# Chunked attention with a gated projection and a feed-forward layer: q and k turned on the host, units of 256 tokens, and a written-out TensorE order

## The chip, the cores and the metric

The kernel runs on one core of a Trainium2 chip. The metric is the device time of one execution in microseconds; before the change the median of three runs is 1155.11 us (1153.89 to 1156.46).

## What is computed

```python
# q, k, v: (8, 8, 576, 64) f32; weights f64 in the reference; B*S = 4608 tokens, 512 channels
scores = scale * matmul(q_c, k_c.T)            # in chunks of 64 tokens, per batch and head
attn   = exp(scores - max) / (sum + 1e-9)
x      = matmul(attn, v_c)                     # heads side by side: (8, 576, 512)

gate = sigmoid(sum_k conv_w[k] * xp[:, k:k+S]) # five taps along the tokens of a batch
y    = (gate * (x @ w_val)) @ w_out

xn  = (y - mu) / sqrt(var + 1e-6) * g_ln
out = y + relu(xn @ w_ch1) @ w_ch2             # 512 -> 2048 -> 512
```

Products are made in three parts of float32r: a number is split into a high part and a remainder (high x high, remainder x high, high x remainder).

## The kernel before, in words

The 4608 tokens are nine blocks (BLK) of 512. Attention works in units (UN) of 128 tokens, two chunks each, so 36 units (NU), four to a block (UPB). A Tile scheduler puts each engine's instructions in order by their place in the source, their readiness and modelled costs; inside `manual_schedule` TensorE keeps the source order and the other engines are still scheduled. `high_priority` draws an instruction forward.

The loop at L703 calls `slot(u)` (L625) for each unit, with stages of different units in one slot. `load_qkv` (L85) loads q, k and v of unit u+2 on SP's queue: q and k with tokens on the partitions, in pieces of 256 bytes, one DMA for each half of the heads and each batch touched (L90), v with four DMAs (L99). `a1` (L182) turns k and q: four TensorE transposes each (L177) into a PSUM tile of the pool `ps_t` (two buffers) and a ScalarE copy to kT or qT (L179). `a3` (L186) makes 32 products of 64x64 for the scores (L193) in the single PSUM tile `sc`, then on VectorE the maximum (L200), the subtraction (L203), after ScalarE's exponential (L207) the sum (L209), the reciprocal (L210) and the multiplication (L212). `a4` (L215) transposes the probabilities of unit u-LAG (L220; LAG is 2) into `ps_t` and ScalarE copies them to pT (L222). `a5` (L242) multiplies them with v (L252, 32 products of 64x64) into the single PSUM tile `x`; ScalarE copies it to xf (L267) and xh (L270), and VectorE makes the remainder xl (L272). Where a batch ends inside the unit, these three are cut in two (`segs`).

The dense work of block j is spread over the slots by the table `dense` (`at`, L684), at two places of a slot (0 behind a1, 1 at the end). `conv` (L277) makes the five taps of one of four channel groups: the first on ScalarE (L282), four on VectorE (L284); the first and the last block do it in two halves. `sigm` (L289) is one ScalarE operation over the block's single tile `cg`, for which the activation table has to be loaded again. `val` (L300) is a chain of twelve products (L298) in one of the two PSUM tiles of `ps_d`, read by gv = product x gate on VectorE (L313), then gh on ScalarE (L316) and gl on VectorE (L317). `proj` (L320) is another chain of twelve, copied out by ScalarE (L330) and stored to a DRAM buffer on ScalarE's queue (L331). A block has four val and four proj.

Weights come as f64 words. `decode` (L105) turns a tile into f32 with one ScalarE and three VectorE operations (L108 to L111); `split` (L113) makes the high part on ScalarE (L116) and the remainder on GpSimd (L117). w_val is decoded behind slot 0, w_out in slots 4 to 8, the first four blocks of the feed-forward weights (`load_ff` L141, `split_ff` L151) at slots 35 to 38 of the source.

TensorE's order is the source's until slot 7 (MANUAL); from there to the feed-forward stage the scheduler's. WARM lists places where `warm` (L617) issues products of the identity. `prep` (L662), behind slot 38, releases the attention pools and starts layer norm for block 0; the feed-forward stage (from L736) follows, again in written-out order.

Of the kernel before, what the change touches and what calls it, by code (L numbers as in the profile page):

```python
# [19 lines left out]
def tile_chunk_attention_gated_mlp(ctx: ExitStack, tc: tile.TileContext, q, k, v, w_val, conv_w, w_out, g_ln, w1, w2, out):  # L20
    nc = tc.nc
    B, H, S, D = q.shape
    DM = H * D
# [8 lines left out]
    UN = 128  # L32
# [7 lines left out]
    LAG = 2  # L40
    EARLY = 3
    MANUAL = 7
    WARM = {(0, 0): 2, (0, 1): 4, (0, 4): 12, (1, 4): 7, (2, 4): 3, (3, 4): 13, (4, 2): 6, (4, 4): 12}
    scale = 1.0 / float(D) ** 0.5
    outf = out.rearrange("b s d -> (b s) d")

    def runs(t0, n):
        done = 0
        while done < n:
            b, s = divmod(t0 + done, S)  # L50
            step = min(n - done, S - s)
            yield done, step, b, s
            done += step
# [9 lines left out]
    ps_t = ctx.enter_context(tc.tile_pool(name="ps_t", bufs=2, space=PSUM))  # L63
# [8 lines left out]
    ps_x = s_a.enter_context(tc.tile_pool(name="ps_x", bufs=1, space=PSUM))  # L72

# [9 lines left out]
    qr, kr, vr = {}, {}, {}  # L83

    def load_qkv(u):  # L85
        for src, dst, nm in ((k, kr, "kr"), (q, qr, "qr")):
            t = pA.tile([P, NP, 2, D], F32, tag=nm, name=nm, bufs=3)
            for off, n, b, s in runs(u * UN, UN):
                for r in range(2):
                    nc.sync.dma_start(  # L90
                        out=t[off:off + n, :, r, :],
                        in_=src[b, NP * r:NP * r + NP, s:s + n, :].rearrange("h p d -> p h d"),
                    )
            dst[u] = t
        t = pA.tile([P, 2, NP, D], F32, tag="vr", name="vr", bufs=6)
        for c in range(2):
            b, s = divmod(u * UN + c * CH, S)
            for r in range(2):
                nc.sync.dma_start(  # L99
                    out=t[CH * r:CH * r + CH, c],  # L100
                    in_=v[b, NP * r:NP * r + NP, s:s + CH, :].rearrange("h k d -> k h d"),
                )
        vr[u] = t
# [60 lines left out]

    exps = [pA.tile([P, NP, 2, CH + 1], F32, name=f"ex{i}", bufs=1) for i in range(2)]
    for t in exps:
        nc.gpsimd.memset(t[:, :, :, CH:CH + 1], 1e-9)
    kT, qT, pt, pT = {}, {}, {}, {}  # L170
# [454 lines left out]
    def slot(u, d0=(), d1=()):  # L625
# [3 lines left out]
        if u < NU:  # L629
            a1(u)  # L630
# [178 lines left out]
```

## Time and profile before

| | |
|---|---|
| median of three runs | 1155.11 us (1153.89 to 1156.46) |
| profiled execution: its span (the profile gives no other time for it) | 1152.2 us |
| share of the span with TensorE busy | 96% |
| share with VectorE busy | 63% |
| share with ScalarE busy | 46% |
| mean granted TensorE clock | 0.985 of full speed |
| DMA packets | 168860, of them 120622 under 512 bytes |
| last value product of attention ends | 324.9 us |

Busy is time in which an engine has at least one instruction in flight; instructions of one engine can overlap by some tenths of a microsecond, so durations added up can be more than the busy time. A matmul's end is modelled, and weight loads (PEld) run beside products. An idle time names what ended it.

### The profile page before, as it was taken

The page shows a single profiled execution, that of the slowest core. Times are in us where ns is not written, and L with a number is a line of the kernel's source. Part 1 is how long each engine was busy: PE and PEld are TensorE (multiplying, and loading weights), DVE is VectorE, ACT ScalarE, POOL GpSimd, SP SyncE. Part 2 cuts the span into 40 slices and gives each one's busy share as a digit, 9 for nine tenths or more (in the row PEclk, how much of TensorE's full clock was granted, in tenths as well). Part 3 has the DMA queues.
Part 4 walks back from the last instruction along what each step waited for, and adds up shares of the span by engine and source line. Part 5 has one row for each costly group of instructions (what it writes and reads, how often), then busy time and mean ns, then how long its engine had stood idle before and what let it go on. Part 6 is the DMA issues. An engine that isn't in the chain of part 4 may idle for free.

```text
span 1152.2 us, 18309 instructions
## 1 busy us (share of the span) xinstructions
PE 1104.5 (96%) x7128; PEld 897.8 (78%) x7128; DVE 722.5 (63%) x1277; ACT 527.1 (46%) x973; POOL 107.8 (9%) x120
## 2 busy tenths in 40 slices
PE   6889999899989899799999999999999999999998
PEld 5678877778768787688887888887888888878877
DVE  6988999989884978545556534446444347432434
ACT  4676777767765665334543223333223324121221
POOL 2010012100002443322220000000000000000000
PEclk8989999999999899999999999999999999999999
DMA  7656677664125672623442623333623222622211
GB/s 185 174 128 161 163 183 211 173 164 115 38 74 169 214 230 80 249 109 110 156 156 89 227 89 126 109 101 100 220 91 129 94 80 92 237 92 83 82 37 73
DMA packets 168860, 155.37 MB, mean 135 GB/s; under 512 B 120622, under 2 KB 128838, under 8 KB 168774
## 3 DMA queue, kind: packets, MB, share of 16 engines
q1 hardware_dynamic: 163590, 144.76, 41.4%
q10 hardware_dynamic: 5184, 9.44, 2.2%
q8 instruction: 56, 0.92, 0.3%
q14 instruction: 30, 0.25, 0.1%
HBM read 116.41 MB, written 37.75 MB: 134 GB/s over the span
## 4 chain that ended last, share of the span: by engine, by line
PE 66%; DVE 18%; ACT 7%; issue 3%; DMA 3%; SPq 1%; POOL 0%; DVEq 0%; ACTq 0%; POOLq 0%
PE acc L530 15%; PE x L556 15%; PE psf L530 14%; PE zy L556 10%; DVE cg L284 4%; PE pso L298 4%; PE psv L298 3%; DVE da L111 2%; DVE da L110 2%; PE acc L416 1%; DMA raw<-in_moe_w_ch 1%; DVE h L568 1%; PE psh L298 1%; PE pst L379 1%; PE x L252 1%
## 5 line engine op out<-in xcount | busy, mean ns | idle before, releaser
L576 DVE TENSOR_TENSOR c<-x,c 128x512 f32<-128x512 f32 x96 | 66.2, 690 | 237.5 <-ACT c L572 181.2
L530 PE MATMUL acc<-w,h 128*128 128x512 f32 x768 | 186.4, 392 | 0.0
L530 PE MATMUL psf<-w,h 128*128 128x512 f32 x768 | 186.0, 391 | 0.0
L530 PEld LDWEIGHTS acc<-w,h 128*128 128x128 f32 x768 | 144.7, 188 | 31.6
L530 PEld LDWEIGHTS psf<-w,h 128*128 128x128 f32 x768 | 144.2, 188 | 31.4
L556 PE MATMUL x<-t,wc 128*128 128x512 f32 x576 | 146.9, 390 | 3.4 <-DVE c L576 3.4
L572 ACT ACTIVATE c<-zy 128x512 f32<-128x512 f32 x96 | 57.9, 604 | 187.5 <-PE zy L556 187.4
L556 PEld LDWEIGHTS x<-t,wc 128*128 128x128 f32 x576 | 108.0, 188 | 27.3 <-DVE c L576 4.3
L567 ACT ACTIVATE h<-c 128x512 fp32r<-128x512 f32 x96 | 60.5, 631 | 137.0 <-DVE c L576 136.4
L284 DVE SCALAR_TENSOR_TENSOR cg<-xf,cw,cg 128x516 f32<-128x516 f32 (+1 forms) x176 | 109.8, 662 | 0.4
L535 DVE TENSOR_TENSOR yt<-psf,yt 128x512 f32<-128x512 f32 x128 | 88.2, 691 | 25.1 <-PE psf L530 21.1
L556 PE MATMUL zy<-b,wc 128*128 128x512 f32 x384 | 99.0, 393 | 0.0
L556 PEld LDWEIGHTS zy<-b,wc 128*128 128x128 f32 x384 | 71.1, 188 | 14.8 <-ACT c L572 0.2
L568 DVE SCALAR_TENSOR_TENSOR h<-c,h 128x512 fp32r<-128x512 f32 x96 | 68.4, 713 | 14.1 <-ACT h L567 13.9
L117 POOL TENSOR_TENSOR w<-da,w 128x512 fp32r<-128x512 f32 x32 | 47.6, 1495 | 155.8 <-ACT w L116 139.3
L298 PE MATMUL psv<-xh,vh 128*128 128x512 f32 x144 | 60.0, 417 | 2.0 <-DVE gv L313 2.0
L298 PE MATMUL pso<-oh,gh 128*128 128x512 f32 x144 | 59.2, 411 | 0.3 <-ACT gh L316 0.3
L298 PE MATMUL psv<-xl,vh 128*128 128x512 f32 x144 | 57.4, 399 | 0.2 <-DVE xl L272 0.2
L298 PE MATMUL pso<-oh,gl 128*128 128x512 f32 x144 | 56.9, 395 | 0.2
L298 PE MATMUL psv<-xh,vl 128*128 128x512 f32 x144 | 57.1, 397 | 0.0
L556 PE MATMUL x<-b,wc 128*128 128x512 f32 x192 | 52.6, 410 | 4.3 <-DVE h L568 3.6
L298 PE MATMUL pso<-ol,gh 128*128 128x512 f32 x144 | 56.4, 391 | 0.0
(114 smaller groups left out, 1711.6 us busy)
## 6 DMA issues: line engine op xcount, KB each, us to landing
wc<-wc SPq DMA_DIRECT2D x112, 512.0 KB, 3.3
raw<-in_moe_w_ch SPq DMA_DIRECT2D x32, 512.0 KB, 4.4
vr<-in_v SPq DMA_DIRECT2D x144, 64.0 KB, 3.1
yd<-y ACTq DMA_DIRECT2D x36, 256.0 KB, 3.3
out<-yt SPq DMA_DIRECT2D x36, 256.0 KB, 3.2
kr<-in_k SPq DMA_DIRECT2D x64, 128.0 KB, 2.9
qr<-in_q SPq DMA_DIRECT2D x64, 128.0 KB, 2.9
yr<-yd SPq DMA_DIRECT2D x32, 256.0 KB, 2.8
```

What stands on the lines that cost most here:

```text
L110: nc.vector.scalar_tensor_tensor(out=au, in0=hw, scalar=0x80000000, in1=au, op0=ALU.bitwise_and, op1=ALU.bitwise_or)
L111: nc.vector.scalar_tensor_tensor(out=au, in0=lw, scalar=29, in1=au, op0=ALU.logical_shift_right, op1=ALU.bitwise_or)
L117: nc.gpsimd.tensor_tensor(out=lo, in0=a, in1=hi, op=ALU.subtract)
L284: nc.vector.scalar_tensor_tensor(out=o, in0=x[:, f, i + lo:i + hi], scalar=cw[:, i * CT + f:i * CT + f + 1], in1=o, op0=ALU.mult, op1=ALU.add,
L298: nc.tensor.matmul(out=ps, lhsT=lt, rhs=rh, start=(i == 0), stop=(i == n - 1))
L530: nc.tensor.matmul(out=ps, lhsT=lt, rhs=rh, start=(g == 0 and k == 0 and (first or half)), stop=(g == 1 and k == 2 and (last or half)),)
L535: nc.vector.tensor_tensor(out=yt[i], in0=ps, in1=yt[i], op=ALU.add)
L556: nc.tensor.matmul(out=ps, lhsT=lt, rhs=rh, start=(start and c == 0 and i == 0), stop=(c == 1 and i == 2), skip_group_check=True)
L567: nc.scalar.activation(out=t[:, 0, :], in_=src, func=ACTF.Relu)
L568: nc.vector.scalar_tensor_tensor(out=t[:, 1, :], in0=src, scalar=0.0, in1=t[:, 0, :], op0=ALU.max, op1=ALU.subtract)
L572: nc.scalar.activation(out=t, in_=zy, func=ACTF.Copy)
L576: nc.vector.tensor_tensor(out=t, in0=x, in1=t, op=ALU.add)
```

## The change

- `kernel` lays q and k out on the host: for each of 18 units of 256 tokens one array of 128 partitions (head half x channel) by 2 (k, q) x 4 heads x 256 tokens, contiguous; v likewise with tokens of a chunk x head half on the partitions. `load_qkv` becomes two DMAs per unit, one of 1 MB for qk and one of 512 KB for v. `a1`, `transpose_in`, `runs`, kT and qT are gone.
- UN is 256: 18 units, two to a block. `a3`, `a4` and `a5` handle twice the tokens per call; `sc`, `x` and the new `ps_p` for the transposed probabilities have one buffer each, of 4 KB per partition. `ps_t` is opened only in `prep`.
- LAG is 1. A slot is scores(u), dense 0, transposes(u-1), dense 1, values(u-1), dense 2 and 3.
- MANUAL is 19: TensorE keeps the source order through slot 18, the last with attention work.
- The dense table is written anew: val of block j at places 2 and 3 of slot 2j+3 and 0 and 1 of slot 2j+4, proj at 2 and 3 of that slot and 0 and 1 of the next. The last block's taps are made at full width. WARM has 70 products where it had 59. w_out is loaded in slot 1 and decoded in slots 2 to 4; the first feed-forward weights stand at slots 17 and 18; the taps' weights (`taps`) are transposed in slot 1.

```diff
-    UN = 128
+    UN = 256
...
-    LAG = 2
-    EARLY = 3
-    MANUAL = 7
-    WARM = {(0, 0): 2, (0, 1): 4, (0, 4): 12, (1, 4): 7, (2, 4): 3, (3, 4): 13, (4, 2): 6, (4, 4): 12}
+    LAG = 1
+    MANUAL = 19
+    NC = UN // CH
+    WARM = {(0, 0): 2, (0, 1): 12, (0, 3): 12, (1, 1): 12, (1, 3): 12, (2, 1): 8, (2, 3): 12}
...
     def load_qkv(u):
...
+        t = qkr[u] = pA.tile([P, 2, NP, UN], F32, tag="qk", name="qkr")
+        nc.sync.dma_start(out=t.rearrange("p a h t -> p (a h t)"), in_=qk[u])
+        t = vr[u] = pA.tile([P, NC, NP, D], F32, tag="vr", name="vr", bufs=3)
+        nc.sync.dma_start(out=t.rearrange("p c h d -> p (c h d)"), in_=v[u])
...
-    def transpose_in(u, src, dst, nm):
-        a = src.pop(u)
-        t = pA.tile([P, NP, UN], F32, tag=nm, name=nm)
-        ps = ps_t.tile([P, NP, UN], F32, tag="t", name="pst")
-        for hp in range(NP):
-            nc.tensor.transpose(out=ps[:, hp, :], in_=a[:, hp].rearrange("p r d -> p (r d)"), identity=ident)
-        with tc.high_priority():
-            nc.scalar.activation(out=t, in_=ps, func=ACTF.Copy)
-            dst[u] = t
-
-    def a1(u):
-        transpose_in(u, kr, kT, "kT")
-        transpose_in(u, qr, qT, "qT")
...
     def a3(u):
-        kt, qt = kT.pop(u), qT.pop(u)
-        sc = ps_s.tile([P, 2, 2 * NP, CH], F32, tag="sc", name="sc")
+        t = qkr.pop(u)
+        kt, qt = t[:, 0], t[:, 1]
+        sc = ps_s.tile([P, 2, NG, CH], F32, tag="sc", name="sc")
...
-        nc.vector.tensor_reduce(out=mx, in_=sc[:, :, 0:NP, :], op=ALU.max, axis=AX.X)
+        nc.vector.tensor_reduce(out=mx, in_=sc, op=ALU.max, axis=AX.X)
...
     def a4(u):
         pr = pt.pop(u)
-        t = pA.tile([P, NP, P], F32, tag="pT", name="pT")
-        ps = ps_t.tile([P, NP, P], F32, tag="t", name="pst")
+        t = pA.tile([P, NG, P], F32, tag="pT", name="pT", bufs=1)
+        ps = ps_p.tile([P, NG, P], F32, tag="p", name="pst")
...
-    def slot(u, d0=(), d1=()):
+    def slot(u):
+        d = [dense.get((u, i), []) for i in range(4)]
         if u + 2 < NU:
             load_qkv(u + 2)
         warm(u, 0)
         if u < NU:
-            a1(u)
+            a3(u)
         warm(u, 1)
-        for fn in d0:
+        for fn in d[0]:
             fn()
         if LAG <= u < NU + LAG:
             a4(u - LAG)
         warm(u, 2)
-        if u < NU:
-            a3(u)
-        warm(u, 3)
+        for fn in d[1]:
+            fn()
         if LAG <= u < NU + LAG:
             a5(u - LAG)
-        warm(u, 4)
-        for fn in d1:
+        warm(u, 3)
+        for fn in d[2] + d[3]:
             fn()
...
     for j in range(NB):
         u = UPB * (j + 1) + LAG - 1
         for f in range(CT):
-            if 0 < j < NB - 1:
-                at(u, [(0, 1), (0, 1), (1, 1), (1, 1)][f], lambda j=j, f=f: conv(j, f, 2))
+            if j == NB - 1:
+                at(u, 3, lambda j=j, f=f: conv(j, f, 2))
+            elif j:
+                at(*[(u, 3), (u, 3), (u + 1, 1), (u + 1, 1)][f], lambda j=j, f=f: conv(j, f, 2))
...
-        at(u, (2, 0), lambda j=j: sigm(j))
+        at(u + 1, 2, lambda j=j: sigm(j))
         for f in range(CT):
-            at(u, [(2, 0), (2, 1), (3, 0), (3, 1)][f], lambda j=j, f=f: val(j, f))
+            at(*[(u + 1, 2), (u + 1, 3), (u + 2, 0), (u + 2, 1)][f], lambda j=j, f=f: val(j, f))
         for t in range(BLK // P):
-            at(u, [(4, 0), (4, 1), (5, 0), (6, 0)][t], lambda j=j, t=t: proj(j, t))
...
+            at(*[(u + 2, 2), (u + 2, 3), (u + 3, 0), (u + 3, 1)][t], lambda j=j, t=t: proj(j, t))
+    for f in range(NFA):
+        at(NU + LAG - 2 + f // 2, 1 + 2 * (f % 2), lambda f=f: early_ff(f))
...
+    for u in range(NU + LAG + 4):
         if u == MANUAL:
             head.close()
-        slot(u, dense.get((u, 0), []), dense.get((u, 1), []))
-        if u == NU + LAG:
+        slot(u)
+        if u == NU + LAG - 1:
             prep()
...
+    def chunks(a):
+        a = np.asarray(a).reshape(8, 2, 4, 9, 64, 64).transpose(0, 3, 1, 2, 4, 5)
+        return a.reshape(18, 4, 2, 4, 64, 64)
+
+    def turned(a):
+        return chunks(a).transpose(0, 2, 5, 3, 1, 4).reshape(18, 128, 1, 4, 256)
+
+    data = {
+        "qk": np.concatenate([turned(inputs["k"]), turned(inputs["q"])], axis=2).reshape(18, 128, 2048),
+        "v": chunks(inputs["v"]).transpose(0, 2, 4, 1, 3, 5).reshape(18, 128, 1024),
+    }
```

## Rows read from the trace of the kernel before

**Rows 1.** Busy time of the engines, from the page

```profile
PE 1104.5 (96%) x7128; PEld 897.8 (78%) x7128; DVE 722.5 (63%) x1277; ACT 527.1 (46%) x973; POOL 107.8 (9%) x120
```

**Rows 2.** Stretches: length, busy of PE, PEld, DVE, ACT, POOL, granted clock, DMA share, GB/s

```profile
0.00:48.00 48.00, 36.80 (x517) 31.49 (x517) 34.79 (x63) 25.18 (x46) 7.02 (x15) 0.93 0.65 159
48.00:73.50 25.50, 18.77 (x253) 15.06 (x252) 24.75 (x50) 20.11 (x35) 5.64 (x5) 0.80 0.78 204
73.50:141.30 67.80, 66.89 (x773) 55.27 (x774) 58.39 (x105) 48.46 (x81) 0.61 (x4) 1.00 0.62 155
141.30:254.80 113.50, 106.41 (x1255) 85.73 (x1254) 108.81 (x199) 84.71 (x143) 12.69 (x14) 1.00 0.68 176
254.80:325.00 70.20, 68.91 (x800) 55.22 (x799) 61.20 (x114) 49.36 (x83) 0.39 (x2) 1.00 0.29 79
```

**Rows 3.** Chain of waits before 330 us: start, length, what

```profile
81.26 0.69 PE x L252 x32
...
84.91 0.87 PE pst L177 x8
...
94.17 2.73 PE psv L298 x12
97.99 1.28 ACT L291
99.28 1.93 ACT cg L291
...
133.16 1.93 ACT cg L291
...
310.30 1.94 ACT cg L291
```

**Rows 4.** Single lines and tiles: durations min/median/max in ns, first and last start

```profile
L291 ACT ACTIVATE cg<-cg x9: 1909/1929/1935, 61.3 to 338.3; 128x2064 f32<-128x2064 f32 x7, 128x2048 f32<-128x2048 f32 x2
...
L143 SPq DMA_DIRECT2D raw<-in_moe_w_ch x16: 378/400/606, 130.8 to 426.2; - x16
...
L298 PE MATMUL psh<-xn,w x192: 390/394/792, 361.3 to 458.6; 128*128 128x512 f32 x192
```

**Rows 5.** Groups of instructions before 325 us: busy us, mean ns, idle before

```profile
L179 ACT ACTIVATE qT<-pst 128x512 f32<-128x512 f32 x36 | 21.4, 594 | 0.5 <-PE pst L177 0.5
L179 ACT ACTIVATE kT<-pst 128x512 f32<-128x512 f32 x36 | 21.3, 591 | 6.5 <-PE pst L177 6.5
...
L111 DVE SCALAR_TENSOR_TENSOR da<-raw,da 128x512 uint32<-128x512 uint32 x19 | 15.7, 824 | 0.1
L110 DVE SCALAR_TENSOR_TENSOR da<-raw,da 128x512 uint32<-128x512 uint32 x19 | 14.0, 739 | 0.2
...
L109 DVE TENSOR_SCALAR da<-da 128x512 uint32<-128x512 uint32 x19 | 7.7, 416 | 10.6 <-ACT da L108 10.6
```

**Rows 6.** Timeline of VectorE in two places: start, length, what

```profile
154.83 4.09 DVE L284 SCALAR_TENSOR_TENSOR cg<-xf,cw,cg 128x516 f32<-128x516 f32 x6
...
349.49 1.22 DVE L424 TENSOR_TENSOR xn<-xt,xn 128x1024 fp32r<-128x1024 f32 x1 [0.97 <-ACT xn L423]
350.64 0.68 DVE L313 TENSOR_TENSOR gv<-psv,cg 128x512 f32<-128x512 f32 x1
351.24 0.68 DVE L317 TENSOR_TENSOR gl<-gv,gh 128x512 fp32r<-128x512 f32 x1
```

**Rows 7.** Timeline of the start, all engines

```profile
7.96 0.73 PE L193 MATMUL sc<-kT,qT 64*64 64x64 f32 x32
...
8.62 2.94 PE L623 MATMUL psw<-ident 128*128 128x128 f32 x24
...
10.62 0.43 DVE L109 TENSOR_SCALAR da<-da 128x512 uint32<-128x512 uint32 x1 [10.62 <-ACT da L108]
```

**Rows 8.** DMA issues, from the page: KB each, median us to landing

```profile
wc<-wc SPq DMA_DIRECT2D x112, 512.0 KB, 3.3
...
raw<-in_moe_w_val SPq DMA_DIRECT2D x4, 512.0 KB, 4.9
```

More of the change, by code (lines that the diff above doesn't have):

```diff
@@ L72, in tile_chunk_attention_gated_mlp @@
     ps_x = s_a.enter_context(tc.tile_pool(name="ps_x", bufs=1, space=PSUM))
+    ps_p = s_a.enter_context(tc.tile_pool(name="ps_p", bufs=1, space=PSUM))
     a_dram = [dram.tile([P, DM], F32, name=f"ad{f}") for f in range(NF)]
@@ L80, in tile_chunk_attention_gated_mlp @@
     gr = const.tile([CT, P], F32, name="gr")
-    qr, kr, vr = {}, {}, {}
+    qkr, vr = {}, {}
     def load_qkv(u):
[L86 to L93, printed above, removed]
-            dst[u] = t
[L95 to L103, printed above, removed]
+        t = qkr[u] = pA.tile([P, 2, NP, UN], F32, tag="qk", name="qkr")
+        nc.sync.dma_start(out=t.rearrange("p a h t -> p (a h t)"), in_=qk[u])
+        t = vr[u] = pA.tile([P, NC, NP, D], F32, tag="vr", name="vr", bufs=3)
+        nc.sync.dma_start(out=t.rearrange("p c h d -> p (c h d)"), in_=v[u])
     def decode(raw, a):
@@ L245, in a5 @@
         va = vr.pop(u)
-        x = ps_x.tile([P, 2, NP, UN], F32, tag="x", name="x")
+        x = ps_x.tile([P, 2, NP // 2, UN], F32, tag="x", name="x")
         for i in range(NP // 2):
-            for c in range(2):
+            for c in range(NC):
+                n, cs = c // 2, slice(c % 2 * CH, (c % 2 + 1) * CH)
                 for f in range(2):
@@ L636, in slot, with at @@
         warm(u, 2)
[L637 to L639 removed]
+        for fn in d[1]:
+            fn()
         if LAG <= u < NU + LAG:
             a5(u - LAG)
[L642 to L657 removed]
+        warm(u, 3)
+        for fn in d[2] + d[3]:
+            fn()
+    dense = {}
+    def at(u, i, fn):
+        dense.setdefault((u, i), []).append(fn)
     s_0 = ExitStack()
[L660 removed]
+    xn0, yt0, ps_t = None, None, None
     def prep():
[L663 removed]
+        nonlocal xn0, yt0, ps_t
         s_a.close()
+        ps_t = ctx.enter_context(tc.tile_pool(name="ps_t", bufs=2, space=PSUM, reuse_waits="tile"))
         p2["b"] = ctx.enter_context(tc.tile_pool(name="p2c", bufs=2, side="right", reuse_waits="tile"))
@@ L681, in prep, with taps, early_ff @@
             high_low(xn0[0][:, :, ts], xn0[1][:, :, ts], p2["xt"][:, :, ts], nc.vector)
-    dense = {}
-    def at(u, pos, fn):
-        dense.setdefault((u + pos[0], pos[1]), []).append(fn)
+    def taps():
+        cwr = stg.tile([KC * CT, P], F32, tag="da", bufs=3, name="cwr")
+        decode(cwu, cwr)
+        ps = ps_p.tile([P, NP * P], F32, tag="p", name="pst")
+        nc.tensor.transpose(out=ps[:, 0:KC * CT], in_=cwr, identity=ident[0:KC * CT, 0:KC * CT])
+        nc.tensor.transpose(out=ps[:, KC * CT:(KC + 1) * CT], in_=gr, identity=ident[0:CT, 0:CT])
+        nc.vector.tensor_copy(out=cw, in_=ps[:, 0:(KC + 1) * CT])
+    def early_ff(f):
+        load_ff(f, stg)
+        split_ff(f, stg)
+    at(0, 3, lambda: split_w("v"))
+    at(1, 0, taps)
+    at(1, 3, lambda: load_w(w_out, "o", CT))
+    for c in range(CT):
+        at([2, 3, 3, 4][c], [3, 0, 3, 0][c], lambda c=c: split_w("o", c, c + 1))
     for j in range(NB):
@@ L784, in tile_chunk_attention_gated_mlp @@
     order.close()
-_INS = ["q", "k", "v", "moe_w_val", "moe_conv_w", "moe_w_out", "moe2_g_ln", "moe2_w_ch1", "moe2_w_ch2"]
+_INS = ["moe_w_val", "moe_conv_w", "moe_w_out", "moe2_g_ln", "moe2_w_ch1", "moe2_w_ch2"]
 _OUT = (8, 576, 512)
```

82 lines of the change are left out of this document (28 added, 54 removed).

## Prediction

> **What bounds the kernel now.** I read the busy times, a table of stretches, the chain of waits, the rows of single tiles, the groups of VectorE and ScalarE, and the two engines' timelines. TensorE is busy for 1104.5 of 1152.2 us [rows 1], but the change touches the part before 325 us alone, where the last product of attention ends, so that part decides. The table [rows 2] has two sorts of stretch. At 73.5 to 141.3 and 254.8 to 325 TensorE leads: busy 98.7% and 98.2%, VectorE 86.1% and 87.2%. At 48 to 73.5 and 141.3 to 254.8 VectorE leads: 97.1% and 95.9%, TensorE 73.6% and 93.8%. The reader should see that both engines are nearly full, and that to lighten one leaves the other. The pace is the distance between sigmoids, one for each block of 512 tokens: 33.9 us where TensorE leads (99.28 to 133.16) [rows 3], 38.0 before it, where VectorE does, and 249 us for the seven blocks from 61.3 [rows 4] to 310.3 [rows 3], 35.6 each. In the long VectorE-led stretch it also decodes feed-forward weights, loaded from 130.8 us on [rows 4].
>
> **What the change removes.** TensorE loses 288 transposes of k and q. In the chain eight of them take 0.87 us [rows 3]; 36 times that is 31.3 us. ScalarE loses 72 copies, 21.3 + 21.4 us [rows 5]; it is busy for at most 79% of any stretch, so this buys no time by itself, only earlier hand-overs. TensorE's idle time in the second stretch, where it waits for k and q, is covered by VectorE at 97%: VectorE is late next there, and I count nothing. SP issues 36 loads of q, k and v where 304 stood; they move the same bytes.
>
> **What merging units does to VectorE.** Four softmax passes run 18 times at 128x1024 where they ran 36 times at 128x512, and the remainder xl goes from 40 instructions to 24 (12 whole units and 6 cut at a batch boundary). That is 72 + 16 = 88 merges. By durations a merge saves 2 x 0.68 - 1.22 = 0.14 us. By starts a 128x512 operation takes 0.60 us of the queue and a 128x1024 one 1.15, both from one run of neighbours [rows 6], so a merge saves 0.05. Instructions overlap where the queue is full, as it is here, so I take the starts: 4.4 us (0 and 12 as bounds). The 18 reciprocals saved are left to the range. The last block's taps become 16 at full width where 32 halves stood, fewer, but none can start before the last product, where half of them could; I set the two against each other.
>
> The Trainium skill, "VectorE: DVE Perf Modes", section "Side-by-side: where the cycles go for N=2048 bf16", adds some 158 cycles of pipe fill and decode to each instruction at 0.96 GHz. By that rule the 88 merges would be worth an estimated 14.5 us instead of 4.4. The trace agrees with it on the duration (0.14 us) and not on the queue (0.05).
>
> **The sum for VectorE.** Busy before 325 us: 34.79 + 24.75 + 58.39 + 108.81 + 61.20 = 287.9 us [rows 2]; less 4.4, 283.5. It starts at 10.62 us, on the first weight, with the first scores behind it [rows 7]. Afterwards the first scores need one load of 1 MB and no transposes or copies. No row shows such a load: 512 KB take 3.3 to 4.9 us [rows 8], so it takes between 3.3 and 9.8. At 5, near the rows, it lands at 6, and VectorE begins near 8 (bounds 6 to 12). TensorE's sum is 36.80 + 18.77 + 66.89 + 106.41 + 68.91 = 297.8 [rows 2], less 31.3, plus eleven more warming products at 0.25 us (24 halves in 2.94) [rows 7]: 269 us. So VectorE becomes the longer engine, and the stage's end is its start, its work and its idle time. It idled for 4.1% of the long stretch that it led, and for 12.8 and 13.9% of those that TensorE led [rows 2]. With TensorE at under 90% of the new stage I take 6.5%, nearer the first: 283.5/0.935 = 303 us, and the end at 311, 14 us earlier. The bounds are 8 + 283.5/0.959 = 304 (21 earlier) and 8 + 283.5/0.861 = 337 (12 later).
>
> TensorE checks this. A block holds eight chains of twelve (2.73 us), 128 score and 128 value products (0.69 us for 32) and sixteen probability transposes (0.44 for four, half of the 0.87): 21.9 + 5.5 + 1.8 = 29.2 us [rows 3]. Seven blocks at 29.2 instead of 35.6 would be 45 us less; VectorE needs about 28.5 of its own per block (58.39/67.8 of 33.9 is 29.2, less 0.5) and the decoding besides, so most of TensorE's gain is not to be had. Between 14 and 45 I stay near VectorE's end, as it is the longer engine: **20 us**.
>
> **What the fixed order and a lag of one add.** TensorE's program becomes scores(u), a dense chain, transposes(u-1), a dense chain, values(u-1), two dense chains. The probabilities of u-1 have a whole slot, about 15 us, for four passes of 1.15 us and an exponential: hidden. The copy of the transposed probabilities is hidden by the 2.73 us chain after them. The tight place is the sigmoid: val(j,0) and val(j,1) fill both dense PSUM tiles, so val(j,2) waits until gv has read val(j,0), which wants all taps and the sigmoid. From the end of block j's values to val(j,2) TensorE has six dense chains, two scores and one value stage of 1.38 us each and transposes: 6 x 2.73 + 3 x 1.38 + 0.87 = 21.4 us. Against it stand the copies out of PSUM (1.2), a first tap (0.6, as a copy of its size), 16 x 0.67 (six in 4.09) [rows 6], xl (1.15), a softmax, if it is put between the taps (4.7), and a table load and the sigmoid (1.28 + 1.93) [rows 3]: 21.6 us. The stall is some 0.2 us a block, none if softmax comes after, and 3 or more if gl and a decoding also go first. It is inside the idle share taken above. A wait on SP is added too: the load of unit u+2 waits for scores(u), with weight loads queued behind it; it has nearly two slots to land and costs nothing unless a load takes over 15 us, against 3.3 to 4.9 [rows 8].
>
> What stands behind 325 us keeps its order; the first feed-forward chain (361.3 us) [rows 4] comes as much earlier.
>
> **The sum.** Span 1152.2 - 20 = 1132.2 us. The median of the three runs, 1155.1, is 2.9 above the span, so the forecast is **1135 us**.
>
> **The rivals.**
> - Merges pay their whole duration (0.14 us): 88 x 0.09 = 8 us more. For it stand the durations, against it the starts. 1127; chance 0.13, in which a denser interleaving is another way to the same number.
> - VectorE's queue idles nearly as where TensorE led, at 9.5%: 8 + 283.5/0.905 = 321, 4 us gained, and up to 8 with the reciprocals. For it: the steps are twice as long, with one set of buffers for scores, values and transposes. 1149; chance 0.17.
> - The gain is not there: the eight decodings of early feed-forward weights are not drawn forward any more, so the stage loses 8 x (0.42 + 0.74 + 0.82) = 16 us of VectorE [rows 5] and the next one, whose first chains want them, gains as much. 1155; chance 0.05.
> - **Slower:** at the sigmoid TensorE can't take other work, as the order is written out. If gl (2 x 0.60) and a decoding (1.98) go ahead of the taps, the stall is 3.4 us a block; if the softmax behind them then misses its own slot, 4.7 more, 8.1. From 6.4 (35.6 - 29.2) on, this costs more than the transposes did: 7 x 1.7 = 12 slower, 1167; chance 0.10. Against it: the trace has six taps in a row [rows 6], so VectorE's order does bring them early.
>
> **How the numbers follow.** The forecast has the other 0.55, with its own range of 1127 to 1143. A measurement here can tell about 0.2% (2.3 us) from nothing. Faster: 0.55 + 0.13 + 0.17 = 0.85; same 0.05; slower 0.10. The range takes in the merge rival, the bounds of the first load and the idling rival, and leaves out the last two: 1116 to 1152, where 1116 is a gain of 39, most of TensorE's 45.
>
> **What would show it.** Right: no transposes of k or q; sigmoids 31 to 34 us apart; VectorE over 92% busy until the last value product near 305; its first pass near 8 us; the first feed-forward chain near 341. Wrong: TensorE waiting on gv for more than 3 us per block, VectorE under 88%, feed-forward weights decoded only after the last block, or a first score after 10 us.

## The result: 0.6% slower, and the profile after

The changed kernel takes 1161.43 us (1159.38 to 1163.26, 5 runs) against 1154.74 (1151.30 to 1156.46, 5 runs) beside it: ratio 1.0063 [1.0045, 1.0082]. Forecast was 1135, with 1152 as the upper end, and a chance of 0.10 for slower.

The busy times of the changed kernel, from the page (answers to [rows 1]):

```profile
PE 1076.1 (93%) x6862; PEld 875.5 (76%) x6862; DVE 714.0 (62%) x1155; ACT 482.4 (42%) x828; POOL 110.6 (10%) x120
```

TensorE lost 28.4 us of busy time, VectorE 8.5 and ScalarE 44.7: what the change removes is gone. DMA packets fell from 168860 to 58581. Yet the span is 1157.6 us, 5.4 longer than before. The stretches of the changed kernel, with the columns of [rows 2], show where TensorE stood still:

```profile
0.00:55.80 55.80, 34.82 (x614) 32.14 (x614) 43.33 (x66) 23.50 (x34) 7.80 (x16) 0.87 0.68 255
55.80:144.00 88.20, 71.40 (x831) 56.80 (x826) 85.28 (x126) 55.72 (x77) 17.01 (x15) 0.91 0.45 152
144.00:322.50 178.50, 160.61 (x1873) 129.37 (x1872) 147.28 (x219) 101.28 (x129) 4.11 (x10) 0.94 0.34 118
322.50:369.50 47.00, 37.36 (x161) 29.86 (x162) 23.50 (x43) 24.81 (x44) 0.00 (x0) 0.89 0.34 115
```

From 55.8 to 144 us VectorE leads (96.7%). From 144 us on, neither TensorE (90.0%) nor VectorE (82.5%) is full; each waits for the other, and the granted clock is below full speed in every stretch, where [rows 2] has 1.00 from 73.5 us on. The sigmoids give the pace (timeline of ScalarE in the changed kernel: start, length, what, and in brackets the idle time before and what ended it):

```profile
66.69 1.91 ACT L257 ACTIVATE cg<-cg 128x2048 f32<-128x2048 f32 x1
...
241.73 1.92 ACT L257 ACTIVATE cg<-cg 128x2064 f32<-128x2064 f32 x1 [3.43 <-DVE cg L250]
275.47 1.92 ACT L257 ACTIVATE cg<-cg 128x2064 f32<-128x2064 f32 x1 [3.43 <-DVE cg L250]
309.13 1.92 ACT L257 ACTIVATE cg<-cg 128x2064 f32<-128x2064 f32 x1 [2.96 <-DVE cg L250]
```

Against [rows 3, 4] the time goes in three places. **The head** loses 5.4 us (first sigmoid 61.3 to 66.69). **The seven blocks** behind it take 242.4 instead of 249.0 us, a gain of 6.6 of the 20 forecast; late blocks take 33.7, as the 33.9 of a TensorE-led block before. **The last block** loses 11.5: its sigmoid stands at 348.62, 39.5 behind the one before it, where it was 28.0. The first feed-forward chain starts at 369.5 (361.3 before), and the stage behind it gives 2.8 back.

The waits of TensorE before 345 us in the changed kernel (engine, tile, what it waited for: total, times, longest; the last block's wait for gv, 7.2 us, ends at 351.3 and is not in them):

```profile
PE psv L264 <- DVE gv L279: 33.9, 8, 6.1
PE pst L645 <- DVE cwr L90: 6.3, 1, 6.3
```

The first is the stall that the prediction priced at 0.2 us a block: a third value chain that waits for gv, as the sigmoid is late. Why it is late, the timeline of VectorE in the changed kernel shows (the first line is ScalarE's, the copy of the block's last values):

```profile
254.82 1.06 ACT L233 ACTIVATE xf<-x 128x512 f32<-128x512 f32 x2
...
255.07 1.28 DVE L283 TENSOR_TENSOR gl<-gv,gh 128x512 fp32r<-128x512 f32 x2
...
256.55 1.23 DVE L179 TENSOR_TENSOR pr<-ex,sm 128x1024 f32<-128x1024 f32 x1
257.70 0.68 DVE L238 TENSOR_TENSOR xl<-x,xh 128x512 fp32r<-128x512 f32 x1
258.30 2.08 DVE L250 SCALAR_TENSOR_TENSOR cg<-xf,cw,cg 128x516 f32<-128x516 f32 x3
...
263.56 1.21 DVE L167 TENSOR_REDUCE mx<-sc 128x16 f32<-128x1024 f32 x1
...
265.36 1.22 DVE L170 TENSOR_TENSOR ex<-sc,mx 128x1024 f32<-128x1024 f32 x1
...
269.16 1.23 DVE L176 TENSOR_REDUCE sm<-ex 128x16 f32<-128x1040 f32 x1
...
271.75 1.22 DVE L179 TENSOR_TENSOR pr<-ex,sm 128x1024 f32<-128x1024 f32 x1
...
273.56 1.22 DVE L238 TENSOR_TENSOR xl<-x,xh 128x1024 fp32r<-128x1024 f32 x1
274.69 0.75 DVE L250 SCALAR_TENSOR_TENSOR cg<-xf,cw,cg 128x516 f32<-128x516 f32 x1
277.43 1.42 DVE L279 TENSOR_TENSOR gv<-psv,cg 128x384 f32<-128x384 f32 x4 [1.99 <-ACT cg L257]
```

Ahead of the first tap (258.30) stand gl and pr; between it and the last (274.69) stand the whole softmax of the unit scored next (263.56 to 271.75) and the xl of the next values (273.56). gv starts at 277.43, 22.6 us after the copy of the last values to xf began (254.82), and takes until 278.80, when TensorE's third value chain starts. Behind the stall comes a second cost, in the same two views of the changed kernel, timeline of TensorE and stretches:

```profile
278.80 0.47 PE L264 MATMUL psv<-xh,vh 128*128 128x512 f32 x1 [3.31 <-DVE gv L279]
...
280.20 0.63 PE L264 MATMUL psv<-xh,vl 128*128 128x512 f32 x1
280.62 0.63 PE L264 MATMUL psv<-xh,vh 128*128 128x512 f32 x1
```

```profile
266.00:275.00 9.00, 9.00 (x140) 7.15 (x142) 9.00 (x13) 4.98 (x6) 0.00 (x0) 1.00 0.31 99
...
278.80:283.30 4.50, 4.50 (x13) 3.44 (x14) 3.51 (x5) 1.04 (x2) 0.00 (x0) 0.62 0.00 0
```

Products that follow each other every 0.23 us at the granted clock of 1.00 (2.4 GHz) are 0.42 apart after 3.3 us of standing still, where the clock is partly at the lower level (1.2 GHz; 0.62 on average). The chain takes 4.58 us instead of 2.75.

### The profile page after: what moved, and what is told of

Its sections match the earlier page's. It is cut to its first block, busy times and chain, and to the rows that moved or that the text cites. A ratio compares the mean times of both kernels' runs of the same rounds, so it can differ in the third digit from the quotient of the medians.

```text
span 1157.6 us, 17062 instructions
## 1 busy us (share of the span) xinstructions
PE 1076.1 (93%) x6862; PEld 875.5 (76%) x6862; DVE 714.0 (62%) x1155; ACT 482.4 (42%) x828; POOL 110.6 (10%) x120
## 4 chain that ended last, share of the span: by engine, by line
PE 62%; DVE 26%; ACT 4%; issue 4%; DMA 3%; POOL 0%; SPq 0%; POOLq 0%; ACTq 0%
PE acc L496 15%; PE x L522 15%; PE psf L496 14%; PE zy L522 9%; DVE cg L250 8%; PE psv L264 5%; DVE da L90 2%; DVE sm L176 2%; DVE da L89 2%; DVE xl L238 1%; DVE gv L279 1%; PE acc L382 1%; DVE mx L167 1%; DVE h L534 1%; DVE ex L170 1%
## 5 line engine op out<-in xcount | busy, mean ns | idle before, releaser
L496 PEld LDWEIGHTS acc<-w,h 128*128 128x128 f32 x768 | 144.2, 188 | 31.4
L496 PEld LDWEIGHTS psf<-w,h 128*128 128x128 f32 x768 | 144.2, 188 | 31.3
L250 DVE SCALAR_TENSOR_TENSOR cg<-xf,cw,cg 128x516 f32<-128x516 f32 (+2 forms) x160 | 105.0, 699 | 0.0
L264 PE MATMUL psv<-xh,vh 128*128 128x512 f32 x144 | 66.0, 458 | 41.1 <-DVE gv L279 41.1
L264 PEld LDWEIGHTS psv<-xh,vh 128*128 128x128 f32 x144 | 31.0, 215 | 49.3 <-issue 28.9
L264 PE MATMUL psv<-xl,vh 128*128 128x512 f32 x144 | 63.1, 438 | 0.0
L264 PE MATMUL psv<-xh,vl 128*128 128x512 f32 x144 | 62.5, 434 | 0.0
```

The lines of the kernel that those rows point to most:

```text
L250: nc.vector.scalar_tensor_tensor(out=o, in0=x[:, f, i + lo:i + hi], scalar=cw[:, i * CT + f:i * CT + f + 1], in1=o, op0=ALU.mult, op1=ALU.add,
L264: nc.tensor.matmul(out=ps, lhsT=lt, rhs=rh, start=(i == 0), stop=(i == n - 1))
L496: nc.tensor.matmul(out=ps, lhsT=lt, rhs=rh, start=(g == 0 and k == 0 and (first or half)), stop=(g == 1 and k == 2 and (last or half)),)
```

## Experiments

Ratios are to the kernel before the change, on the same chip. Edits are to the changed kernel unless another is named.

### The layout alone

The kernel before, with its units of 128, its lag and the scheduler's order, but q, k and v loaded in the new layout:

```diff
+        t = qkr[u] = pA.tile([P, 2, NP, UN], F32, tag="qk", name="qkr", bufs=3)
+        nc.sync.dma_start(out=t.rearrange("p a h t -> p (a h t)"), in_=qk[u])
...
-        if u < NU:
-            a1(u)
```

> The kernel before with one part of the change: q, k and v laid out on the host and loaded with two DMAs per unit, no transposes of k and q, no copies; units of 128 tokens, a lag of two, the scheduler's TensorE order from slot 7 on, as before. Theory (the fixed order at the sigmoid ate what the transposes gave back): 31 us of TensorE are gone and nothing was added, so sigmoids come 31 to 32 us apart where TensorE led (33.9 before), and the time is 10 to 18 us below before, 1137 to 1145. Rival (VectorE was the bound, the transposes were covered): within 4 us of before.

1158.03 us, ratio 1.003 [1.0009, 1.0051]: slightly slower, and within the rival's 4 us. TensorE fell to 1089.0 us busy, but waited 21.8 us in ten for the probabilities, at a mean granted clock of 0.966 (before 0.985). So the transposes' 31 us can be lost without units of 256 or a written-out order. A lag of three took most of that wait away, and a source order besides told whether the scheduler was to blame:

```diff
-    LAG = 2
+    LAG = 3
```

> The kernel before with the host layout alone (1158.0 us, where TensorE waited 21.8 us in 10 for the probabilities), and the probabilities used three units later instead of two. Theory (without the transposes of k and q TensorE reaches the probabilities before VectorE has made them; the loss is one of latency): waits for pr under 8 us, sigmoids from block 4 on 32 to 34 apart, time 1144 to 1152. Rival (VectorE's sum sets the pace, 29 to 36 us a block, so TensorE waits somewhere else): the waits move to gv or the scores, time within 4 of 1158. Third (one more unit of lag at the end costs a block's tail): time over 1160.

1153.96 us, 0.9985 [0.9955, 1.0014]: 4 us better. The wait for pr fell from 21.8 to 4.6 us, the waits at the score tile rose from 17.9 to 26.3 in all, and late blocks still took 33 to 37. Mostly the rival: the wait moved.

```diff
-    LAG = 2
-    MANUAL = 7
+    LAG = 3
+    MANUAL = 39
```

> The kernel before with the host layout alone, a lag of three, and TensorE's instructions in source order through the last unit. With a lag of three and the scheduler's order TensorE waited 4.6 us for the probabilities, but 26 us at the score tile, and took 34 us a block. Theory (the order that the scheduler found is what kept the layout's gain away): waits at the score tile under 8 us, blocks 5 to 8 at 31 to 32.5, time 1138 to 1148. Rival (the written-out order stalls here as it did in the changed kernel, behind the sigmoid): waits for gv over 15 us, time 1152 to 1162.

1178.69 us, 1.0209 [1.0176, 1.0242]. The rival holds, and more than it said. Waits of TensorE in this kernel:

```profile
PE psv L272 <- DVE gv L287: 40.8, 8, 10.5
```

The stall of the changed kernel, in another kernel with small units: it comes with the fixed order ahead of the sigmoid. That some order gives the layout alone its gain was not shown.

### The order on TensorE

```diff
-    MANUAL = 19
+    MANUAL = 5
```

> The changed kernel with the scheduler's TensorE order from slot 5 on instead of slot 19. Theory: at a late sigmoid the scheduler lets TensorE take other work, the waits on gv (33.9 us in 8 waits) shrink to under 10, sigmoids come 31 to 32 us apart instead of 33.7, and the time falls by 10 to 20 us to about 1145. Rival (units of 256 with one set of buffers and a lag of one make the stage latency-bound in any order): 1158 to 1165, the waits stay or move to other tiles.

1152.41 us, 0.9985 [0.9968, 1.0001], 9.0 below the changed kernel, between theory and rival. Waits for gv fell from 33.9 to 12.4 us, but 13.0 us of waits for pT came in. The order was a cause, not the whole.

### The taps ahead of the next softmax

```diff
-                at(*[(u, 3), (u, 3), (u + 1, 1), (u + 1, 1)][f], lambda j=j, f=f: conv(j, f, 2))
+                at(u, 3, lambda j=j, f=f: conv(j, f, 2))
```

> The changed kernel, with all four channel groups' taps of a block (2 to 8) placed at the end of its own slot, ahead of the next unit's softmax in the source; TensorE's program is the same. Theory (the sigmoid is late because 4.7 us of softmax stand between the taps on VectorE): the wait on gv falls from 3.3 us to below 1 in blocks 4 to 8, sigmoids come 30.5 to 32 us apart, 1140 to 1150. Rival (VectorE is the longer engine by its sum of work, or softmax then comes late itself): the wait goes from gv to pr, the pace stays at 33 to 34 us and the time within 5 us of 1161.

1153.13 us, 0.9992 [0.9976, 1.0008], 8.3 below the changed kernel with the same TensorE program. Its waits before 345 us:

```profile
PE pst L186 <- DVE pr L179: 23.6, 8, 4.5
PE psv L264 <- DVE gv L279: 14.2, 3, 7.1
```

The last value product ended 8 us earlier (313.9). What gv lost, pr partly took: with softmax behind the taps, the transposes wait for it. (The 14.2 hold the last block's wait, 7.1 us, which here ends ahead of 345; the 33.9 of the changed kernel don't hold its 7.2.) The time lies between theory and rival.

### Layer norm behind the last sigmoid

In the changed kernel `prep` stands one slot before the last sigmoid. Its timeline of ScalarE:

```profile
338.39 2.93 ACT L337 ACTIVATE yt<-yt,w,r 128x512 f32<-128x512 f32 x4 [4.15 <-DVE w L335]
341.23 4.20 ACT L347 ACTIVATE xt<-pst,cw 128x128 f32<-128x128 f32 x16
345.21 2.10 ACT L389 ACTIVATE xn<-xt 128x1024 fp32r<-128x1024 f32 x2
...
348.62 1.91 ACT L257 ACTIVATE cg<-cg 128x2048 f32<-128x2048 f32 x1
```

The taps are done at 339.9; layer norm's 9 us go first.

```diff
-        if u == NU + LAG - 1:
+        if u == NU + LAG:
             prep()
```

> The changed kernel with layer norm of block 0 (prep) one slot later in the source, behind slot 19, as before it stood one slot behind the last values. Theory (at the end ScalarE does the layer norm's scaling and 18 copies ahead of the last block's sigmoid, 348.6 us where the taps end at 339.9): the sigmoid comes near 342, the first feed-forward chain 5 to 8 us earlier than 369.5, the time 4 to 8 us below the changed kernel, 1153 to 1157. Rival (the feed-forward stage is held by its weights anyway): within 2 us of 1161.

1156.76 us, 1.0025 [1.0008, 1.0041]: 4.7 less than the changed kernel, sigmoid at 343.25. Together with the taps:

> Two of the earlier edits together: the taps placed ahead of the next softmax (measured 1153.1 alone) and prep one slot later (1156.8 alone, where the changed kernel has 1161.4). Theory (two separate losses, one at each block's sigmoid and one at the last block's): they add up, 8 + 5 us, to about 1148; the last sigmoid comes near 332 instead of 340.6 and the first feed-forward chain near 356. Rival (once the stage is shorter the feed-forward stage is held by its weights, so the second edit is worth nothing any more): within 2 us of 1153.

1147.93 us, 0.9949 [0.9931, 0.9968]: the two add up (8.3 + 4.7 = 13.0; 13.5 measured).

### The head

The timeline of TensorE in the changed kernel shows the transposes of the taps' weights, put ahead of the first probabilities, waiting for their decoding:

```profile
26.66 0.29 PE L645 MATMUL pst<-ident,cwr 20*128 20x20 f32 x1 [6.35 <-DVE cwr L90]
...
30.39 1.88 PE L219 MATMUL x<-pT,vr 64*64 64x64 f32 x60 [1.11 <-ACT pT L188]
```

```diff
-    at(1, 0, taps)
+    at(1, 3, taps)
```

> The changed kernel with the turning of the conv taps' weights (two TensorE transposes that wait 6.4 us for their decoding) behind the first unit's value products instead of ahead of its probability transposes. Theory (written-out order: the first values, 30.4 us, wait for something that they do not need, and VectorE idles 4 us for them): the first values come near 24, the first sigmoid 3 to 5 us earlier than 66.7, the time 2 to 5 us below 1161. Rival (VectorE is full at 40 to 100 us, so the head's wait is made up there): the first sigmoid moves by less than 1.5 us, the time by less than 1.5.

1155.73 us, 1.0005 [0.9989, 1.002]: 5.7 less than the changed kernel; first values at 25.7, first sigmoid at 60.89. With all three edits:

> The three edits of order together: taps ahead of the next softmax, prep one slot later, the conv weights turned behind the first values. Theory: the losses add, 8 + 5 + 3 us, about 1145, clearly below the kernel before (1154.2). Rival (the losses overlap: what one stage gains the next gives back waiting for VectorE): 1150 to 1154.

1143.45 us, 0.9908 [0.9888, 0.9928]: 18.0 less, and 8.3 + 4.7 + 5.7 is 18.7.

### The tail, and the one gate tile

The run with three edits still took 36.4 us for the last block. The last block's taps in halves, as before the change:

```diff
-                at(u, 3, lambda j=j, f=f: conv(j, f, 2))
+                at(u - 1, 3, lambda j=j, f=f: conv(j, f, 0))
+                at(u, 3, lambda j=j, f=f: conv(j, f, 1))
```

> Three losses undone, and the last block's taps in two halves again, as before the change. In the run with three losses undone the last sigmoid was at 328.2 us, 36.4 behind the one before, against 28.0 in the kernel before the change. Theory (the halves matter: the first half of the taps runs while the last unit is still being computed): sigmoid near 320 to 322, first feed-forward chain near 343 to 345, time 1136 to 1139 against 1143.5. Rival (the forecast's 'the two set against each other': the last products or layer norm set the sigmoid): sigmoid at 326 to 328, time within 2 of 1143.5.

> As the run with halves, and layer norm of block 0 one more slot later in the source. Theory (layer norm's instructions on VectorE, about 6 us between taps, and four on ScalarE, 2.9 us ahead of the table load, still delay the last sigmoid): sigmoid 3 to 6 us earlier than with halves alone, and 2 to 4 us off the time, so 1133 to 1136. Rival (layer norm's result is then late for the first feed-forward chain): that chain is not earlier, or later by some us, and the time is equal to or above that with halves alone.

1139.56 us, 0.989 [0.9854, 0.9927], and with layer norm yet later 1138.46, 0.987 [0.984, 0.99]: 3.9 and 5.0 less than the run with three edits, but longer than the theories had it (last sigmoids in the profiles at 331.8 and 324.7 us). In both, the first half of block 8's taps is written into `cg` while two value chains of block 7 have yet to read their gate, so those rows come from another gate; in the changed kernel's table the halves can't stand without a second gate tile. That is why full width was not merely "set against" the halves. A third use of xf's two buffers gives the tile:

```diff
+        if j == NB - 1 and j not in cgs:
+            cgs[j] = pD2.tile([P, CT, BLK + 2 * HALO], F32, tag="xf", name="cg8")
+        o = cgs.get(j, cg)[:, f, lo:hi]
```

> Three losses undone, the last block's taps in two halves into a gate tile of their own (a third use of the two buffers of xf, so that block 7's gate stays whole for its last two value chains), and layer norm of block 0 one slot later. Theory (the tail was late because the last block's taps could not start before the last values, and they could not because the one gate tile was in use): last sigmoid at 322 to 326, first feed-forward chain near 344 to 346, time 1136 to 1140, as the run where the halves were written over block 7's gate (1138.5). Rival (the spare tile comes free late, as block 7's taps and halo copy still read it): sigmoid at 328 or later, time 1142 to 1145.

1138.54 us, 0.9871 [0.9842, 0.9899]: theory. Timeline of ScalarE in this kernel:

```profile
298.59 1.69 ACT L250 ACTIVATE cg<-xf,cw 128x256 f32<-128x256 f32 x4
...
320.75 1.92 ACT L260 ACTIVATE cg<-cg 128x2048 f32<-128x2048 f32 x1
322.57 1.50 ACT L340 ACTIVATE yt<-yt,w,r 128x512 f32<-128x512 f32 x2
```

The last block's taps start at 298.59 (309.94 in the run with three edits), ahead of the last values, which end at 307 to 308 in both. The last sigmoid now stands ahead of layer norm's yt, 29.7 us behind the one before, and the first feed-forward chain at 343.7. Without the written-out order (MANUAL = 5):

> The run with the spare gate tile, and TensorE's order left to the scheduler from slot 5 on. Theory (the written-out order cost something only because of the three losses; with them gone it is as good as the scheduler's): time within 3 of that run. Rival (the scheduler's order is better here too, as it was by 9 us in the changed kernel): 5 us or more below it. Third (the scheduler puts attention's stages back to back and TensorE waits at the score tile, as with the layout alone): 5 us or more above it.

1141.41 us, 0.989 [0.9854, 0.9926], 2.9 more: theory, just. The written-out order is no loss once these pieces are moved.

### A later place for the transposes of the probabilities

```diff
-        if LAG <= u < NU + LAG:
-            a4(u - LAG)
-        warm(u, 2)
         for fn in d[1]:
             fn()
+        if LAG <= u < NU + LAG:
+            a4(u - LAG)
...
```

In the run with three edits, `a4`, `a5` and the whole dense table go one chain later.

> Three losses undone, and the transposes of the probabilities and the value products each one dense chain later in a slot, with the dense table shifted along. TensorE waited there for pr 21.7 us in 7 and for gv 10.9 us in 3. Theory (TensorE comes to these transposes too early; 2.7 us more of slack takes most of each wait): waits for pr under 8 us, pace of blocks 2 and 3 still about 35 because VectorE is full there, time 1134 to 1140. Rival (the loop of softmax, values, taps and sigmoid is as long as before, so the wait only moves): waits for gv grow by what those for pr lose, time within 3 of 1143.5. Third (the dense window between a block's values and its third projection is what counts; it is the same): no change.

1153.18 us, 0.9994 [0.9976, 1.0012]: 9.7 more than without the edit, and the wait for pr stayed (28.0 us in nine). All three expectations missed; from the third on the sigmoids came 33 to 38 us apart. The place of `a4` didn't make the slack, perhaps since everything behind it moved along; why it lost so much is open.

### What a stall costs besides its wait

Identity products ahead of each third value chain of blocks 0 to 7, in the place of the wait:

```diff
+    def fill():
+        ps = ps_p.tile([P, NG, P], F32, tag="p", name="psw")
+        for _ in range(22):
+            nc.tensor.matmul(out=ps[:, 0, :], lhsT=ident, rhs=ident, start=True, stop=True)
+    for j in range(NB - 1):
+        at(2 * j + 4, 0, fill)
```

> The changed kernel with 22 more products of the identity in a PSUM tile of their own ahead of each val(j,2), where TensorE waits 3 to 6 us for gv; nothing waits for them but TensorE itself. Theory (the wait also costs the clock: the chain behind it takes 4.4 to 5.4 us instead of 2.75, at a granted clock of 0.83 to 0.91 in such stretches): the products take 2.7 us of the wait, the chain behind it falls to 2.75 to 3.5 us, sigmoids in blocks 4 to 8 come 32 us apart instead of 33.7, and the time falls by 6 to 12 us, to 1150 to 1155. Rival (the slow chain is bookkeeping, or gv itself sets the pace): the pace stays at 33.7 or grows by what the products take, 1160 to 1172.

1159.27 us, 1.004 [1.0023, 1.0057], 2.2 less. Timeline of TensorE in this kernel:

```profile
276.75 5.18 PE L661 MATMUL psw<-ident 128*128 128x128 f32 x44
281.68 0.48 PE L264 MATMUL psv<-xh,vh 128*128 128x512 f32 x1
```

The chain ran at full speed (2.79 us), but the fill outlasted the wait, and the chain started 7.6 us behind its sigmoid (274.12) instead of 3.3. So this run could not tell. With 11 products (`range(11)`):

> The changed kernel with 11 identity products ahead of each third value chain, where 22 took 4.9 to 5.2 us in place of a wait of 3.1 to 4.4 us and so pushed the chain back by more than they spared. Eleven take about 2.6 us, less than the wait, so the chain starts when gv is read, as in the changed kernel. Theory (the lower granted clock behind the wait, 4.4 to 5.4 us for a chain that takes 2.75 at the full one, is on the path that sets the pace): chains at 2.8 us, pace of blocks 5 to 8 32 to 32.5 instead of 33.7, time 1148 to 1153. Rival (the chain's slowness is absorbed later, by the wait of the next block): chains at 2.8 us, the next wait longer by as much, pace 33.5 to 33.9, time 1158 to 1163. Third (the fill does not hold the clock): chains at 4.4 us, no change.

1148.46 us, 0.9955 [0.9939, 0.9972]: **13.0 less than the changed kernel (12.5 by the ratios), by adding useless work**. Timeline of TensorE, and stretches between two sigmoids, in this kernel:

```profile
238.50 2.72 PE L661 MATMUL psw<-ident 128*128 128x128 f32 x22
240.98 0.48 PE L264 MATMUL psv<-xh,vh 128*128 128x512 f32 x1
```

```profile
205.40:236.80 31.40, 31.40 (x392) 26.03 (x391) 28.21 (x43) 19.25 (x25) 0.31 (x2) 1.00 0.41 135
236.80:268.20 31.40, 31.40 (x392) 25.99 (x392) 28.11 (x42) 19.29 (x26) 0.31 (x2) 1.00 0.40 135
```

In these blocks TensorE never stops; a block takes 31.4 us where it took 33.7, at a granted clock of 1.00. By its time it is the theory, with a pace a little shorter still. The last five blocks are 2.0 to 2.4 us shorter each, 11.1 together; the first four keep waits for gv of 0.6 to 3.7 us and gain little.

But the fill did not change the clock alone. With it in TensorE's order the scheduler made another order on ScalarE: the next exponential goes ahead of the copy to pT, which stands behind the slow chain. Timeline of ScalarE behind the sigmoids at 275.47 (changed kernel) and 236.83 (this run):

```profile
284.28 1.03 ACT L188 ACTIVATE pT<-pst 128x1024 f32<-128x1024 f32 x1 [4.45 <-PE pst L186]
...
287.14 1.06 ACT L174 ACTIVATE ex<-ex 128x1024 f32<-128x1024 f32 x1
```

```profile
244.36 1.06 ACT L174 ACTIVATE ex<-ex 128x1024 f32<-128x1024 f32 x1 [1.93 <-DVE ex L170]
...
245.85 1.01 ACT L188 ACTIVATE pT<-pst 128x1024 f32<-128x1024 f32 x1
```

The exponential comes 7.5 us behind its sigmoid instead of 11.7, so softmax is done sooner and the next taps meet less other work on VectorE. Of a late block's 2.3 us, the chain gives 1.6 (2.84 from its start to the next stage, instead of 4.39) and the way from the block's values to the end of the next sigmoid 1.6 (21.4 instead of 23.0), and 0.8 is lost as the chain starts 0.8 later behind its sigmoid. The first is the clock's. How much of the second comes from the faster chain and how much from the new order, no run separates.

The Trainium skill, "TensorE: Matmul & The Clock Gate", section "Loop structure matters more than you think", says that the loop nest decides whether products run at the full clock, with a wait for a DMA as its example. Here TensorE waits for VectorE, and the two runs agree: 0.62 granted behind the 3.3 us wait, 1.00 with the fill in its place.

Then the short fills where VectorE leads, ahead of `a4` in the run with the spare gate tile:

```diff
+        for _ in range(8):
+            nc.tensor.matmul(out=ps[:, 0, :], lhsT=ident, rhs=ident, start=True, stop=True)
+    for u in (6, 8, 10):
+        at(u, 0, fill)
```

> The run with the spare gate tile, and 8 filling products (2.0 us) ahead of the transposes of the probabilities in slots 6, 8 and 10, where TensorE waits 4.9, 5.3 and 3.1 us for pr and the transposes behind the wait take 1.57 to 1.97 us instead of 1.04. Theory (the granted clock behind these waits is on the path): each block 2 to 4 gains 1 to 2.5 us, time 1132 to 1136. Rival (VectorE is full in these blocks, 31.7 of 32, 36.6 of 38 and 35.4 of 37 us, so a faster TensorE only waits longer): within 2 of 1138.5.

1136.73 us, 0.9843 [0.9809, 0.9877]: 1.8 less, inside the rival's bound (3.2 less by the ratios). In this kernel's timeline the transposes stayed slow at the first two places (1.97 us without the fill):

```profile
106.47 1.94 PE L186 MATMUL pst<-ident,pr 128*128 128x128 f32 x8 [3.22 <-DVE pr L179]
```

So it did not tell whether the clock counts there; a wait of 3.2 us was left behind the fill. At the third place 1.5 us of wait were left, the transposes ran at a granted clock of 1.00 (0.69 without the fill), and the sigmoid behind them came 31.4 us after the one before instead of 32.3.

### The best version

The run with the spare gate tile, with the taps back where the change put them, and 11 fills ahead of the third value chain:

```diff
-                at(u, 3, lambda j=j, f=f: conv(j, f, 2))
+                at(*[(u, 3), (u, 3), (u + 1, 1), (u + 1, 1)][f], lambda j=j, f=f: conv(j, f, 2))
...
+    for j in range(NB - 1):
+        at(2 * j + 4, 0, fill)
```

> The run with the spare gate tile, but with the taps where the change put them (half of them behind the next scores) and 11 filling products ahead of the third value chain. The changed kernel gained 13.0 us from these fills alone, and from the head, the tail and layer norm about 15 us together. Theory (the losses are at different places and add up): blocks 5 to 8 at 31 to 32, last sigmoid near 320, time 1132 to 1136. Rival (with the fills TensorE's program is 31.9 us a block, against 30.2 to 32 with the taps drawn ahead): time 1138 to 1144.

1133.79 us (1130.51 to 1135.71), 0.9815 [0.9781, 0.9848]: it beats both kernels. The losses were at different places and add up. Busy times and sigmoids of this kernel:

```profile
PE 1083.9 (96%) x7038; PEld 885.9 (78%) x7038; DVE 717.1 (63%) x1171; ACT 484.5 (43%) x832; POOL 112.0 (10%) x120
```

```profile
228.30 1.93 ACT L260 ACTIVATE cg<-cg 128x2064 f32<-128x2064 f32 x1 [1.15 <-DVE cg L252]
259.63 1.93 ACT L260 ACTIVATE cg<-cg 128x2064 f32<-128x2064 f32 x1 [1.18 <-DVE cg L252]
291.23 1.93 ACT L260 ACTIVATE cg<-cg 128x2064 f32<-128x2064 f32 x1 [1.49 <-DVE cg L252]
315.76 1.92 ACT L260 ACTIVATE cg<-cg 128x2048 f32<-128x2048 f32 x1
```

Late blocks take 31.3 to 31.6 us, the last one 24.5, and TensorE is at 96% again.

## Why the prediction was wrong, by its own steps

**The sums of work were near.** TensorE's program of a block is 31.4 - 2.5 of fill = 28.9 us (29.2 forecast). VectorE's work up to the last value product is 43.33 + 85.28 + 147.28 = 275.9 us, under the 283.5 forecast; 3.5 us of the difference is work that now lies behind that point. The 20 us of gain itself was no sum: it was taken between VectorE's 14 and TensorE's 45.

**VectorE as the longer engine, with 6.5% of idle time: wrong behind 144 us.** Up to there it leads (96.7%), as forecast; in the long stretch behind it is 82.5% busy. From its first instruction (9.03) to 322.5 us it idles for 37.6 us, 12.0%, where the sum took 19.7. The 6.5% was read off stretches in the scheduler's order; that the written-out order and one buffer each for scores, values and transposes make the difference is argued: the scheduler's order gave 9.0 us back, and no run has a second buffer. Two engines at 90 and 82% mark a loop of hand-overs, and such a loop has to be summed along its path, not per engine.

**"The stall is some 0.2 us a block": the failed step.** The path was looked for in the right place (21.4 us of TensorE against copies, taps, softmax and sigmoid), but its sum of 21.6 us ended with the sigmoid. In the block shown above it is 0.5 us until the copy of the values starts, 22.6 from there to gv, and 1.4 that gv itself takes, a term that the sum did not have: 24.5 against 21.2 of TensorE, a wait of 3.3. Of the case named for 3 us and more, gl did come ahead of the taps; in place of a decoding stood pr, and the next xl between the taps. The measured waits are 3.1 to 6.1 us, 33.9 in all. The step then counted them as "inside the idle share".

**"The first feed-forward chain ... comes as much earlier": failed too.** The last value product ends 2.4 us earlier (322.5 against 324.9), the first feed-forward chain starts 8.2 us later. So of the 25.4 us between the forecast's span and the measured one (1132.2 and 1157.6) 17.6 arose ahead of the last values and 10.6 between them and that chain, and the feed-forward stage gave 2.8 back. Of the signs of being wrong, the waits for gv over 3 us and VectorE under 88% (85.5% up to 322.5 us) came.

**What had no term:** the chain behind the wait at the lower clock, 1.6 to 2.6 us at each of eight places. The short fills gained 13.0 us; the faster chain is 1.6 of a late block's 2.3 us, and the rest isn't separated from the new order that came with them. The rows that could have warned were there: [rows 2] grants 0.80 in the only stretch with TensorE at 74%.

**The head and the tail: not costed.** The taps' weights in slot 1 (5.7 us) and `prep` ahead of the last sigmoid (4.7) are moves in the order, named in the change, for which the prediction has no term. Halves against full width, set against each other, were worth about 5 us together with a later layer norm (1143.45 to 1138.54), with the taps starting before the last values.

**The merges.** VectorE lost 8.5 us of busy time over the whole kernel with 122 instructions fewer. By starts 88 merges were 4.4 us; the other 34 instructions are 18 reciprocals and 16 taps of the last block, left to the range.

By the Trainium skill, "VectorE: DVE Perf Modes", section "Side-by-side: where the cycles go for N=2048 bf16", 122 instructions at 158 cycles and 0.96 GHz are an estimated 20 us; the measured 8.5 says that in a full queue most of that fixed part overlaps.

**The rival.** "Slower: at the sigmoid TensorE can't take other work" named the place and the stall, and gave 1167 against a measured 1161. That the number is near is luck: it made each block longer than before, 12 us in all, and the seven blocks are 6.6 us shorter; the loss lies in the head (5.4) and the last block (11.5), which it doesn't name. Its chance of 0.10 was argued down with six taps in a row [rows 6], which was another order: there, TensorE was not written out, and the taps were not split around the next scores. The rival without any gain is out: all 19 decodings stand before 177 us, and 19 stood before 325 [rows 5]. The first load, which the range bounded at 3.3 to 9.8 us, allowed the first scores at 5.8 us.

The forecast's 1135 was reached, at 1133.8, only with three misplaced pieces moved (the weights of the taps, layer norm, the last taps) and the fills; it is no sign that the sum was right.

## What to carry to other kernels

When an order is written out by hand, sum the whole path of hand-overs from one use of a shared tile to the next, with everything the other engine may put in between, and compare it with the work that stands in the fixed order meanwhile; the busy sums alone say nothing. A wait on TensorE costs more than its length where the granted clock falls behind it, and more so if the slow work lies on the loop that ends in the next wait: filling the wait with useless products, shorter than the wait, gained 1.1% here. An added instruction can also change the order that a scheduler gives the other engines, so compare their timelines before the gain is put down to one cause. When work is taken off the leading engine, check what each moved line (a weight's transposes, a layer norm, a full-width last block) now stands ahead of, at the head and at the tail.

## What was not expected of the hardware

Removing work made the kernel no faster even without any other change: with 31 us of transposes gone (the layout alone), the mean granted clock fell from 0.985 to 0.966. Adding work made it faster: 11 identity products per block, 2.5 us at eight places, took 13.0 us off. In a late block 3.3 us of wait and 1.8 us of slower products vanished together, with 2.5 us of filling in their place, and the pace went from 33.7 to 31.4 us, though with another order on ScalarE too.
